# Another order of all steps in an attention and gated-MLP kernel

## The chip, the cores and the metric

One core of a Trainium2 chip runs the whole kernel. The metric is the device time of one execution in microseconds, taken as the median of several runs.

## The reference, cut to what matters

Chunked attention over 4 batches, 8 heads, 768 positions and 64 features; then a gated MLP over the 512 features, whose gate mixes the 768 positions. All in fp32.

```python
for c in range(nc):                       # 24 chunks of 32 queries
    k_ctx = k[:, :, l_start:r_end]        # 16 keys to the left, 8 to the right
    k_full = np.concatenate([mem_k, k_ctx], axis=2)
    scores = scale * np.matmul(q_c, k_full.transpose(0, 1, 3, 2))
    a = softmax(scores)
    out[:, :, c_start:c_end] = np.matmul(a, v_full)
x = attn_out.transpose(0, 2, 1, 3).reshape(B, S, H * D)
h = gelu(x @ w_in)
u, v = h[..., :d_ff // 2], h[..., d_ff // 2:]
v_n = (v - mu) / np.sqrt(var + 1e-06) * g_ln
v_s = np.einsum('ts,bsd->btd', w_sg, v_n) + b_sg[None, :, None]
return x + (u * v_s) @ w_out
```

## The kernel before, in words

The work is cut into some 1,200 named steps. Each step belongs to one engine, or may be put on either of two (a star after its name picks the second). The string ORDER (line 35) lists all steps, and the loop at line 565 issues them in that order. Every engine runs its own steps strictly in the order of the string; semaphores are set by the tiles that a step reads and writes. So the string alone sets the queue of each engine and which buffer a step gets.

The matrix products are made of two fp32r parts each (a high part and the rest), three products for one: low by high, high by low, high by high (`HL`).

- Weights. `r` loads a block of 128 rows of w_in (i) or w_out (o) as 64-bit words, `d1` to `d6` turn it into a high part (`d5`) and a low part (`d6`). i10 to i13 are the four blocks for the V products, i00 to i03 those for the U products. `g`, `ga`, `gb` load and split w_sg. `cb` loads g_ln (in pieces of 4 bytes) and b_sg; `cbh` halves them.
- Attention, for each of 24 tiles of 128 positions (u = 0 to 23, six to a batch): `q`, `k`, `v` load, `S` is the score product (64 small matmuls in the trace, PSUM tile `s`, one buffer), then `mx`, `sb` (VectorE), `ex` (ScalarE), `sm`, `sr`, `nm`. For u < 10 `T` transposes on TensorE and `p` copies; for the others `yt` transposes on VectorE and four `E` steps exchange blocks by 16 DMAs, for two tiles together. `A` is the value product (PSUM tile `av`, one buffer); `xc`, `xh`, `xl` copy it out, as fp32, high and low part.
- MLP, for each batch b: `V` (6 products, by tile), `v1` to `v9` are gelu, layer norm and split (`v1` to `v4` read PSUM; the result lies in one of two `g` buffers from `v1` to `v9`); `U` (8 products), `u1` to `u4` gelu; `W` (8 products, each over all six V results of the batch), `w1` to `w4` scale, gate and split; `O` (8 products), `o1` adds x, `out` stores.
- V, U, W, O and T share four PSUM banks `mm`, given out in the order of the string.
- `zz n` are n warm-up matmuls on a zeroed tile whose result nobody reads.

Names: S13 is the score product of tile 13; V14 is batch 1, tile 4; U103 is batch 1, half 0, column block 3; v714 is step v7 of V14.

The SP queue issues all DMAs in the order of the string; each issue may wait for its buffer.

```python
def warm(n):
    for _ in range(n if mms.free else 0):
        tensor.matmul(mms.free[0], still[:, 0, 0:P], still[:, 1], start=True, stop=True)
```

Of the kernel before, what the change touches and what calls it, by code (L numbers as in the profile page):

```python
# [45 lines left out]
p5 g00 d3o0 xh4 U001 q9 v801 mx7 z6 k9 vy02 gb20 xl4 sb7 v901 u1003 A5 sm6 ex7 u2003 v602 v103 S8 v8 sr6 sm7
nm6* u3003 V04 v203 xc5 k10 q10 xh5 sr7 mx8 v303 xl5 ga11 v403 ga00 gb11 u4003 V05 v503 u1001 v702 u2001 v802
vx03 gb00* u3001 sb8 v902 T6 u4001 ex8 S9 p6 gb01* v104 sm8 nm7* U011 q11 k11 mx9 vy03 v204 v603 sb9 v703*
v304 T7 sr8 u1011 v404 A6 p7 nm8 v803 U013 v504 ex9 v9 v903 xc6 u2011 vx04 sm9 u3011 vy04 v105 v604 u4011 T8
u1013 sr9 v704* v205 A7 p8 u2013 v305 nm9 U010 xc7 v10 v405 v804 u3013 gb50* v505 T9 v904* u1010 A8 u2010 d1o0  # L50
# [5 lines left out]
O003 mx12 w3011 sb12 w4011 k14 q14 ex12 O001 Eb5 o1003 z12 sm12 sr12 nm12 O011 o1001 out003 Ed5 O002 o1011
out011 out001 O013 o1002 yt12 out002 O010 o1013 out013 S13 o1010 out010 O000 mx13 q15 k15 sb13 ex13 S14 sm13
xh6 xh8 o1000 O012 k16 sr13 xh7 mx14 xl8 out000 q16 xl7* xl6* V11 nm13 o1012 yt13 out012 xc9 sb14 xh9 V10 ex14
xl9 v111 sm14 v211 sr14 v311 nm14 S15 v411 v110 v511 A10 q17 v210 k17 U102 vx11 mx15 xc10 v13 vy11 v611 v310
sb15 xh10 v410 ex15 xl10* V13 u1102 v510 u2102 vx10 sm15 u3102 vy10 v610 u4102 sr15 V14 v710 v711 v810 v811  # L60
# [20 lines left out]
yt23 w3213 w1201 w4213* w2201 A20 w1203 w3201 w4201* W212 xc20 v23 w2203 w3203 w4203 O202 w1212 w2212 w3212
w4212 A21 o1202 out202 O200 Eb11 O203 o1200 Ea11 W210 o1203 out200 out203 Ec11 O201 w1210 w2210 Ed11 w3210
w4210* W211 xh19 o1201 xh20 xl19 out201 xh18 xl20* xl18 V31 w1211 w2211 xc21 w3211 w4211* O212 v131 v231 v331
O211 v431 o1212 v531 out212 vx31 V30 vy31 o1211 v631 out211 v731 v831 v931* A22 v130 v230 O210 xc22 v330 v430
v530 U303 o1210 vx30 out210 vy30 v630 v730 U300 u1303 v830 u2303 v930* u3303 u4303 O213 u1300 u2300 u3300
# [548 lines left out]
```

## Time and profile before

| what | us |
|---|---|
| median of 3 runs | 397.53 (397.05 to 400.51) |
| profiled execution | 396.41 |
| its span, first to last instruction | 394.6 |
| TensorE busy in the span | 375.0 |
| VectorE, ScalarE, GpSimd busy | 268.0, 155.0, 111.3 |

In the profile PE is TensorE, PEld its weight loads, DVE VectorE, ACT ScalarE, POOL GpSimd, SPq the queue that issues DMAs. Nearly every step has line 105, since one helper records them all; a group is told by its tiles. Ends of matmuls are modelled, so starts are the better measure for them.

### The profile page before, as it was taken

Reading aid. Unit: us, or ns where it says so; the run is one execution under the profiler, and the core shown is the slowest. Engines: PE = TensorE matmul, PEld = TensorE weight load, DVE = VectorE, ACT = ScalarE, POOL = GpSimd, SP = SyncE. Lnnn points to the kernel's source line nnn. Section 1 sums busy time; section 2 is a strip of 40 time slices with the busy share of each in tenths; the row PEclk is TensorE's granted clock in tenths of the full one; section 3 lists DMA queues with packets and bytes.
Section 4 is the critical chain, followed back from the end, with each engine's and each line's share of the span. In section 5 each row is a group of like instructions: output and inputs, shape, how many; then the busy total and the mean of one; then the engine's idle time right before and its main releaser. Section 6 shows DMA issues by size and latency. Waiting matters only on the chain.

```text
span 394.6 us, 11079 instructions
## 1 busy us (share of the span) xinstructions
PE 375.0 (95%) x4787; PEld 343.7 (87%) x4787; DVE 268.0 (68%) x489; ACT 155.0 (39%) x288; POOL 111.3 (28%) x132
## 2 busy tenths in 40 slices
...
GB/s 261 404 398 218 275 227 182 175 281 119 1 122 168 122 120 64 107 128 154 95 193 156 75 75 3 98 37 67 73 87 96 42 33 9 2 0 0 2 78 83
DMA packets 24528, 47.64 MB, mean 121 GB/s; under 512 B 4384, under 2 KB 13600, under 8 KB 24480
## 3 DMA queue, kind: packets, MB, share of 16 engines
q1 hardware_dynamic: 24480, 46.94, 36.2%
...
HBM read 36.96 MB, written 6.29 MB: 110 GB/s over the span
## 4 chain that ended last, share of the span: by engine, by line
PE 69%; DVE 9%; POOL 7%; DMA 6%; ACT 4%; issue 2%; SPq 2%; DVEq 0%; ACTq 0%; POOLq 0%
PE mma L105 16%; PE mmc L105 16%; PE mmd L105 15%; PE mmb L105 13%; PE av L105 6%; PE s L105 3%; POOL gb L105 2%; SPq L105 2%; DMA rawe<-in_w_in 2%; POOL ga L105 2%; DMA ub<-in_w_sgT 2%; DVE ga L105 2%; DMA ka<-in_ks 1%; DVE paira L105 1%; DVE gb L105 1%
## 5 line engine op out<-in xcount | busy, mean ns | idle before, releaser
L105 ACT ACTIVATE eb<-eb 128x512 f32<-128x512 f32 x12 | 7.6, 631 | 31.4 <-DVE eb L105 31.1
L105 DVE STREAM_TRANSPOSE y<-na 128x512 f32<-128x512 f32 x14 | 9.9, 707 | 6.9 <-DMA pt<-y 3.2
L105 PE MATMUL s<-ka,qa 64*32 64x64 f32 x768 | 10.5, 224 | 3.9 <-DMA ka<-in_ks 2.0
L105 DVE SCALAR_TENSOR_TENSOR mmc<-mmc,g_half,b_half 128x384 f32<-128x384 f32 x11 | 6.8, 621 | 10.7 <-PE mmc L105 10.7
L105 PEld LDWEIGHTS s<-ka,qa 64*32 64x32 f32 x768 | 8.5, 105 | 6.4 <-issue 3.9
L105 PEld LDWEIGHTS av<-pt,vb 64*64 64x64 f32 x512 | 8.8, 134 | 5.8 <-issue 2.5
L105 PE MATMUL av<-pt,vb 64*64 64x32 f32 x512 | 9.8, 221 | 3.5 <-ACT xa L105 1.5
L105 PE MATMUL mma<-w_in_hi,paira 128*128 128x512 f32 x40 | 11.1, 399 | 1.8 <-DVE paira L105 1.8
L105 PE MATMUL mma<-vhf 128*128 128x512 f32 x34 | 10.6, 469 | 2.4 <-POOL vhf L105 2.4
L105 PEld LDWEIGHTS s<-kb,qb 64*32 64x32 f32 x768 | 8.4, 105 | 3.5 <-issue 1.7
L105 PEld LDWEIGHTS mma<-vhf 128*128 128x128 f32 x34 | 7.6, 233 | 4.2 <-POOL vhf L105 2.3
L105 ACT ACTIVATE ea<-ea 128x512 f32<-128x512 f32 x12 | 7.6, 632 | 9.4 <-DVE ea L105 9.4
L105 PE MATMUL s<-kb,qb 64*32 64x64 f32 x768 | 10.5, 224 | 0.7 <-issue 0.7
L105 PEld LDWEIGHTS av<-pt,va 64*64 64x64 f32 x512 | 8.5, 134 | 3.0 <-issue 1.8
L105 PE MATMUL av<-pt,va 64*64 64x32 f32 x512 | 9.5, 221 | 1.2 <-issue 0.8
L105 PEld LDWEIGHTS mma<-w_in_hi,paira 128*128 128x128 f32 x40 | 7.3, 187 | 3.6 <-DVE paira L105 2.1
L105 PEld LDWEIGHTS av<-pt,vc 64*64 64x64 f32 x512 | 8.4, 134 | 2.0 <-issue 1.3
L105 PE MATMUL mma<-w_in_hi,pairb 128*128 128x512 f32 x32 | 8.9, 400 | 1.1 <-DVE pairb L105 1.1
L105 ACT ACTIVATE gb<-gb 128x512 f32<-128x512 f32 x12 | 7.6, 633 | 5.4 <-DVE gb L105 5.4
L105 ACT ACTIVATE ga<-ga 128x512 f32<-128x512 f32 x12 | 7.6, 633 | 5.4 <-DVE ga L105 5.4
L105 DVE SCALAR_TENSOR_TENSOR mmd<-mmd,g_half,b_half 128x384 f32<-128x384 f32 x8 | 5.0, 624 | 6.9 <-PE mmd L105 6.9
L105 PE MATMUL av<-pt,vc 64*64 64x32 f32 x512 | 9.4, 221 | 0.1
(520 smaller groups left out, 1235.2 us busy)
## 6 DMA issues: line engine op xcount, KB each, us to landing
...
pt<-y SPq DMA_DIRECT2D x112, 32.0 KB, 1.9
...
```

Source lines behind the costliest of these rows:

```text
L105: return self.tc.keep_in_program_order(getattr(self.engine, name)(*args, **kw))
```

## The change: another string

Only ORDER changes; the steps are the same. Of the steps that may go on either of two engines 88 change their engine, so VectorE runs 473 steps instead of 489 and GpSimd 138 instead of 122. The warm-up matmuls are 56 instead of 43, in seven pieces. Cut to its beginning and the lines that the text speaks of:

```diff
-g40 ri10 ri13 g10 q0 k0 ri12 k1 g30 d2i10 d1i10 q1 d3i10 d4i10 d2i13* g50 ri00 d1i13 d3i13 d5i10 ri11 d4i13
-d6i10* d5i13 zz17 S0 v0 d6i13 mx0 d2i12* q2 sb0 d1i12 k2 d3i12 ex0 ri02 d4i12 zz9 S1 v1 z0 d5i12 sm0 ri01
-d6i12 mx1 sr0 sb1 d1i00 k3 nm0 d2i00* ex1 d1i11* q3 zz8 T0 d2i11* sm1 p0 sr1 v2 d3i00 zz2 A0 g31 d3i11 d4i00
-xh0 S2 ri03 d4i11 xc0 d5i00 xl0 nm1* q4 d5i11 mx2 d1i02 d6i00 zz4 T1 sb2 d2i02* p1* ex2 d6i11* zz3 A1 k4 sm2
-d3i02 V00 xc1 g51 sr2 d1i01 d2i01 nm2 g41 xh1 d3i01 v3 d4i02 T2 d4i01 d5i02 ro0 S3 p2 xl1 d5i01 A2 mx3 v100
-d6i02 k5 sb3 V01 xh2 v200 xc2 q5 d2i03 v300 xl2 cb ex3 d3i03 d1i03 v400 V02 v101 d4i03 v500 d5i03 v5 sm3 d6i03
-v4 v201 vx00 sr3 S4 v301 d6i01* v401 vy00 ga40 U000 q6 v600 ga31 mx4 ga30 k6 nm3 d2o0* v501 gb30 ga10 T3 ga51
-sb4 ga41 U002 gb10 vx01 g01 ex4 p3 gb40* g21 ga50 sm4 gb51 g20 S5 sr4 v700 u1000 A3 gb31* k7 v800 u2000 q7
...
-vx05 u4013 u3010 vy05 ro1 S10 v605 p9* xc8 v11 v705 U012 k12 u4010 q12 v805 mx10 d4o0 A9 sb10 d5o0 v905* ex10
-S11 v12 d6o0* d1o1 sm10 W012 q13 mx11 k13 d2o1 sb11 sr10 d3o1 ex11 nm10 ro2 W003 w1012 z11 sm11 d4o1 sr11 d5o1
...
-v713* u1101 u4103 u2101 vx14 u3101 vy14 v614 v813 u4101 v714 A11 v913 v814 S16 xc11 v14 v914* Ed6 v112 U100
-mx16 xh11 v212 xl11* v312 sb16 V15 k18 u1100 v412 Eb6 ex16 u2100 v512 u3100 sm16 vx12 u4100 U113 Ea6 vy12 v115
...
-w2100 W113 q21 mx19 v16 w3100 q20 w4100* k20 u1110 Ed7 u2110 u3110 W102 w1113 u4110 k21 w2113 Ea7 w2110 w3113
-w3110 w4113 W103 w1102 w4110* w2102 w3102 w4102* yt16 W111 w1103 nm17 w2103 sb19 w3103 yt17 w4103 ex19 S20
...
-out102 Ea8 O111 o1112 out112 O101 o1111 out111 yt18 nm19* O110 o1101 yt19 out101 sb21 nm20 O100 ex21 o1110
-sm21 out110 sr21 S22 o1100 xh12 xh13 out100 xl12* O113 xh14 xl13 mx22 xl14* sb22 V22 o1113 ex22 out113 xc15
...
-u1212 u4211 v824 u2212 v525 u3212 v924* U213 u1210 vx25 u4212 vy25 v625 u2210 yt20 u3210 v725 A18 u4210 v825
-nm21 S23 xc18 v21 v925 yt21 A19 mx23 nm22* sb23 W213 xc19 Eb10 ex23 z23 sm23 sr23 Ed10 W202 w1213 Ec10 W200
...
-v933* V35 u1302 v434 u3301 u2302 v534 u3302 u4301 u4302 U311 v135 vx34 vy34 v634 v235 v734 v335 U310 v834 v435
...
-u3312 W300 u4312 W303 w1300 w2300 w3300 w4300* u1313 u2313 W311 w1303 u3313 w2303 u4313 w3303 w4303 W301 w1311
...
+k1 ri12 q0 k0 g00 g31 q1 ri13 g30 d2i12 d1i12 ri11 d3i12 v0 d4i12 d5i12 zz18 S0 ri01 d6i12 g11 mx0 k2 sb0 g01
+ex0 zz5 S1 z0 mx1 d1i13 q2 d2i13 sm0 ri10 d3i13 sr0 d4i13 d1i11 v1 sb1 d5i13 nm0 ex1 k3 d2i11 zz17 T0 sm1
+d6i13 p0 sr1 zz2 A0 d3i11 d2i01* q3 nm1 ri03 d1i01 d3i01 T1 xc0 d4i11 cb xh0 d4i01 p1 d5i11 zz3 S2 ri00 xl0
+d5i01 d6i11* mx2 d6i01 d1i10 q4 d2i10* sb2 zz5 A1 v2 d3i10 ex2 d4i10 ri02 sm2 d5i10 xc1 sr2 d6i10 xh1 zz6 S3
+k4 xl1* nm2* V00 mx3 d1i03 q5 d2i03 v3 sb3 cbh g50 ex3 sm3 d2i00* g21 T2 sr3 V01 d1i00 k5 d3i03 p2 d3i00 v100
+d4i03 v200 nm3* d5i03 ro0 A2 v300 d4i00 v101 v400 v4 d6i03 T3 d2i02* v201 xh2 S4 v5 d1i02 v500 xc2 xl2 p3 vx00
+d3i02 V02 d5i00 q6 mx4 vy00 v301 v600 sb4 d6i00 k6 v401 ex4 d4i02 A3 sm4 d5i02 v700 S5 xc3 v6 sr4 d6i02* v800
+q7 mx5 nm4* U000 ga01 k7 v501 d2o0* v900 ga30 sb5 ga31 vx01 ex5 d3o0 T4 ga50 U001 gb30* v102 gb01* ga21 g10
...
+d5o0 v705 A7 d6o0 v805 S9 xc7 v10 v905 A8 mx9 q11 k11 sb9 d1o1* W000 xc8 v11 ex9 sm9 d2o1 sr9 d3o1 nm9 ro2
...
+ex15 v211 sm15 v311 sr15 v411 A10 v112 v511 S16 v212 xc10 v13 vx11 v312 A11 vy11 mx16 k18 v611 q18 v412 V10
...
+sb17 u3103 yt15 ex17 u4103 nm16* U111 z17 v114 sm17 v214 sr17 v314 V15 u1111 v414 u2111 v514 u3111 u4111 vx14
...
+u3100 u4100 W103 Ec7 Eb7 W111 w1103 w2103 w3103 w4103 v16 u1102 W101 w1111 u2102 w2111 u3102 w3111 u4102 yt16
+w4111* W113 w1101 nm17* w2101 yt17 w3101 sb19 nm18* ex19 S20 w4101* sm19 A14 q22 w1113 k22 sr19 w2113 W112
...
+yt19 xh14 o1101 xh12 sb21 xh13 out101 xl14* ex21 xl13 S22 o1111 sm21 out111 V22 mx22 sr21 nm20 xc15 xl12* xh15
+sb22 V21 xl15 v122 ex22 v222 sm22 v322 sr22 v422 V20 v522 v121 v221 vx22 v321 vy22 v622 v421 v722* A16 v521
+vx21 S23 xc16 v19 vy21 v822 A17 v621 mx23 xh16 v721 V23 xl16* xc17 v20 Ed9 v821 v922* xh17 v921* v120 xl17
+v220 V24 Eb9 v320 v123 v420 v223 v520 v323 Ea9 vx20 v423 U212 vy20 v620 v523 v720* Ec9 V25 u1212 u2212 v820
+vx23 vy23 u3212 v623 u4212 v920 U200 v723 v124 v823 v224 v923 U202 v324 yt20 u1200 v424 nm21* v125 u2200 U211
...
+u3211 A18 u1201 sr23 v525 u4211 U213 v824 v21 vx25 u2201 xc18 vy25 v625 u4202 u3201 v924* u4201 v725* U203
+u1213 yt21 u2213 u3213 nm22* v825 u4213 A19 u1203 v925 u2203 U210 xc19 Ec10 u3203 u4203 W210 Eb10 Ea10 W201
...
+V35 v833 v434 u1303 v933 v534 u2303 vx34 u3303 vy34 v634 u4303 U310 v135 v734 v235 v834 v934* v335 U312 v435
...
+u3311 W313 u4311 W311 w1313 W310 w1311 w2311 w3311 w4311 u1313 W302 w1310 u2313 w2310 u3313 w3310 u4313 w4310*
...
```

## Rows read from the trace of the kernel before

**Rows 1.** The page, part 1: busy time, share of the span and instructions of each engine.

```profile
PE 375.0 (95%) x4787; PEld 343.7 (87%) x4787; DVE 268.0 (68%) x489; ACT 155.0 (39%) x288; POOL 111.3 (28%) x132
```

**Rows 2.** Windows of 2 us: PE, PEld, DVE, ACT, POOL busy; clock, DMA, GB/s.

```profile
26.00:28.00 2.00, 1.45 (x24) 1.23 (x25) 2.00 (x6) 0.85 (x2) 0.00 (x0) 0.77 1.03 391
...
28.00:30.00 2.00, 2.00 (x6) 1.61 (x5) 1.04 (x2) 1.34 (x3) 1.10 (x1) 0.50 1.06 391
...
36.00:38.00 2.00, 2.00 (x10) 1.60 (x9) 2.00 (x5) 1.65 (x4) 0.00 (x0) 1.00 0.65 90
```

**Rows 3.** Timeline of TensorE, start to 60 us: start, duration, what, idle before.

```profile
10.47 0.85 PE L105 MATMUL s<-ka,qa 64*32 64x64 f32 x64 [2.00 <-DMA ka<-in_ks]
...
26.55 0.55 PE L105 MATMUL av<-pt,vb 64*64 64x32 f32 x22 [1.26 <-issue]
...
27.02 2.04 PE L105 MATMUL mmc<-w_in_hi,paira 128*128 128x512 f32 x4
...
40.76 0.97 PE L105 MATMUL mmd<-paira,w_in_lo 128*128 128x384 f32 x4
...
42.97 0.60 PE L105 MATMUL mmc<-ident,na 128*128 128x128 f32 x4
```

**Rows 4.** Timeline of the other engines, start to 25 us; the same columns.

```profile
14.09 0.69 DVE L105 TENSOR_REDUCE rda<-ea 128x8 f32<-128x520 f32 x1
...
14.72 0.69 DVE L105 TENSOR_REDUCE mxb<-s 128x8 f32<-128x512 f32 x1
...
18.45 1.28 POOL L105 TENSOR_TENSOR na<-eb,rdb 128x512 f32<-128x512 f32 x1
...
18.75 1.53 DVE L105 SCALAR_TENSOR_TENSOR exb<-rawb,exb 128x512 int32<-128x512 int32 x1
```

**Rows 5.** Chain that ended last, in order of time: start, us, what.

```profile
8.72 6.81 DMA rawe<-in_w_in
...
27.09 4.54 PE mmc L105 x12
...
37.24 2.80 PE mmb L105 x12
...
40.04 0.79 PE s L105 x53
...
46.44 1.06 PE av L105 x64
...
101.22 3.18 PE mma L105 x18
...
118.00 2.08 PE mmc L105 x12
```

**Rows 6.** Windows of 40 to 80 us and of 85 to 391 us; columns as in rows 2.

```profile
40.00:80.00 40.00, 39.70 (x975) 35.11 (x978) 38.77 (x76) 30.93 (x62) 28.82 (x32) 1.00 0.65 208
...
85.00:391.00 306.00, 298.63 (x3135) 279.96 (x3128) 196.53 (x357) 100.02 (x186) 69.86 (x81) 1.00 0.26 80
```

**Rows 7.** Timeline, 79 to 82 us: U012 on TensorE and v705 on VectorE.

```profile
80.19 0.55 DVE L105 TENSOR_SCALAR gb<-gb,mvc,rsc 128x512 f32<-128x512 f32 x1
...
80.22 0.96 PE L105 MATMUL mma<-pairb,w_in_lo 128*128 128x384 f32 x4
```

**Rows 8.** Timeline of TensorE after 150 us: rows ahead of which it sat idle.

```profile
158.55 0.73 PE L105 MATMUL mma<-w_in_hi,pairb 128*128 128x512 f32 x2 [1.13 <-DVE pairb L105]
...
194.97 0.86 PE L105 MATMUL s<-ka,qa 64*32 64x64 f32 x64 [1.06 <-DVE eb L105]
...
225.56 0.73 PE L105 MATMUL mma<-w_in_hi,paira 128*128 128x512 f32 x2 [1.82 <-DVE paira L105]
...
266.50 1.14 PE L105 MATMUL av<-pt,vb 64*64 64x32 f32 x64 [1.50 <-ACT xa L105]
```

**Rows 9.** Timeline, 228 to 238 us: first and last step after V22.

```profile
228.65 0.60 ACT L105 ACTIVATE gb<-mma 128x512 f32<-128x512 f32 x1 [0.75 <-PE mma L105]
...
236.48 0.69 DVE L105 TENSOR_TENSOR vhc<-gb,vhc 128x512 fp32r<-128x512 f32 x1 [0.36 <-ACT vhc L105]
```

More of the change, by code (lines that the diff above doesn't have):

```diff
@@ L46 @@
[L46 to L50, printed above, removed]
@@ L56 @@
[L56 to L60, printed above, removed]
@@ L71 @@
-out102 Ea8 O111 o1112 out112 O101 o1111 out111 yt18 nm19* O110 o1101 yt19 out101 sb21 nm20 O100 ex21 o1110
-sm21 out110 sr21 S22 o1100 xh12 xh13 out100 xl12* O113 xh14 xl13 mx22 xl14* sb22 V22 o1113 ex22 out113 xc15
-sm22 xh15 sr22 xl15* A16 v122 v222 U201 xc16 v19 v322 xh16 v422 xl16 v522 V21 u1201 vx22 u2201 vy22 v622 u3201
-v722* u4201 V23 v121 v822 v221 v922* v321 v421 U200 v521 v123 v223 vx21 v323 vy21 v621 V20 v423 u1200 v721*
-u2200 u3200 v821 u4200 v921* U202 v120 v220 v320 A17 u1202 v420 u2202 U203 xc17 Ea9 v520 u3202 vx20 xh17 v523
@@ L76 @@
-vy20 v620 u4202 v720* V24 xl17* u1203 v20 u2203 Ec9 vx23 v820 vy23 v623 u3203 v920 u4203 V25 Ed9 v723* v124
-v224 v823 v324 v923* U211 Eb9 v424 v125 v524 v225 U212 u1211 vx24 v325 vy24 u2211 v624 v425 u3211 v724 U210
-u1212 u4211 v824 u2212 v525 u3212 v924* U213 u1210 vx25 u4212 vy25 v625 u2210 yt20 u3210 v725 A18 u4210 v825
-nm21 S23 xc18 v21 v925 yt21 A19 mx23 nm22* sb23 W213 xc19 Eb10 ex23 z23 sm23 sr23 Ed10 W202 w1213 Ec10 W200
-w1202 w2202 Ea10 w3202 w4202 u1213 W201 w1200 v22 u2213 w2200 u3213 yt22 w3200 w4200* u4213 W203 nm23 w2213
@@ L81 @@
[L81 to L85, printed above, removed]
@@ new lines @@
+q7 mx5 nm4* U000 ga01 k7 v501 d2o0* v900 ga30 sb5 ga31 vx01 ex5 d3o0 T4 ga50 U001 gb30* v102 gb01* ga21 g10
+xh3 v202 z5 g51 gb31 ga00 xl3* p4 gb00 sm5 g41 S6 ga11 v302 sr5 nm5 V03 g20 k8 v402 gb50 mx6 vy01 q8 u1001
+v502 gb11 u2001 gb21 u1000 vx02 T5 sb6 u3001 A4 u2000 ex6 vy02 g40 v601 u4001 ga10 z6 S7 u3000 v701* v7 sm6
+xc4 u4000 U003 k9 ga51 mx7 q9 xh4 sr6 p5 sb7 gb10 ga20 xl4 v801 U002 gb20* u1003 v901* ex7 u2003 ga40 v602
+v103 sm7 gb51 S8 u3003 v203 u1002 gb40 u4003 A5 ga41 k10 mx8 v303 q10 v702* sr7 V04 v403 xc5 v8 xh5 u2002 v503
@@ new lines @@
+u3002 xl5 v802 gb41* u4002 V05 v902* vx03 nm6 v104 vy03 v204 v603 sb8 v304 U011 v703 ex8 v404 v803 sm8 v903
+v504 T6 u1011 sr8 U012 vx04 p6 nm7* u2011 v105 u3011 vy04 v205 v604 u4011 v305 T7 v704 A6 u1012 v405 nm8* v804
+u2012 U013 xc6 v9 v505 u3012 v904* u4012 d1o0* p7* T8 u1013 vx05 U010 p8 u2013 vy05 ro1 d4o0 u3013 v605 u4013
+d5o0 v705 A7 d6o0 v805 S9 xc7 v10 v905 A8 mx9 q11 k11 sb9 d1o1* W000 xc8 v11 ex9 sm9 d2o1 sr9 d3o1 nm9 ro2
+W011 w1000 d4o1 w2000 d5o1 w3000 d6o1 W001 w1011 w4000 d1o2 w2011 d2o2 w3011 d3o2 u1010 u2010 ro3 d4o2 u3010
@@ new lines @@
+W003 w1001 d5o2 u4010 d6o2* w2001 w4011* w3001 S10 w4001 w1003 d1o3 w2003 T9 q12 mx10 W002 k12 w3003 p9* sb10
+w4003* ex10 d2o3 sm10 S11 d3o3 w1002 A9 k13 sr10 w2002 q13 nm10* mx11 w3002 W012 v12 w4002* yt10 sb11 d4o3
+ex11 d5o3 z11 sm11 S12 d6o3 w1012 W013 k14 mx12 q14 w2012 sb12 w3012 sr11 w4012 ex12 nm11* S13 w1013 z12 yt11
+O001 q15 k15 mx13 Ea5 sm12 sb13 O003 o1001 ex13 sr12 w2013 nm12* Ec5 sm13 w3013 w4013* O002 o1003 sr13 out003
+Ed5 S14 o1002 W010 mx14 sb14 out002 ex14 out001 sm14 Eb5 sr14 S15 w1010 w2010 O000 mx15 k17 w3010 q16 w4010*
@@ new lines @@
+k16 q17 O011 o1000 xh7 xh6 out000 xl7* xh8 xl6 yt12 V11 o1011 xl8 out011 nm13 yt13 V12 xc9 sb15 nm14* v111
+ex15 v211 sm15 v311 sr15 v411 A10 v112 v511 S16 v212 xc10 v13 vx11 v312 A11 vy11 mx16 k18 v611 q18 v412 V10
+xc11 v14 v711 Ed6 v512 v811 sb16 v911 vx12 ex16 sm16 vy12 U101 Eb6 v612 v110 sr16 v712 v210 v812 v310 v912*
+O010 u1101 v410 Ea6 u2101 v510 u3101 O013 u4101 o1010 vx10 out010 vy10 v610 Ec6 O012 v710 o1013 v810 v910
+out013 U103 o1012 xh11 xh10 out012 xl11 xh9 xl9* S17 xl10 u1103 yt14 A12 q19 mx17 k19 nm15* V14 u2103 v15 xc12
@@ new lines @@
+sb17 u3103 yt15 ex17 u4103 nm16* U111 z17 v114 sm17 v214 sr17 v314 V15 u1111 v414 u2111 v514 u3111 u4111 vx14
+vy14 U110 v115 v614 v714 v215 v814 v315 v914 V13 u1110 v415 u2110 v515 u3110 u4110 vx15 S18 v113 vy15 v615
+v213 U113 q20 k20 v715 v313 mx18 v815 v413 U112 v915* u1113 v513 sb18 vx13 u2113 ex18 vy13 S19 v613 u1112 z18
+u3113 A13 v713* u2112 q21 mx19 k21 u3112 U100 u4113 xc13 Ed7 u4112 sm18 v813 sr18 v913* U102 u1100 Ea7 u2100
+u3100 u4100 W103 Ec7 Eb7 W111 w1103 w2103 w3103 w4103 v16 u1102 W101 w1111 u2102 w2111 u3102 w3111 u4102 yt16
@@ new lines @@
+w4111* W113 w1101 nm17* w2101 yt17 w3101 sb19 nm18* ex19 S20 w4101* sm19 A14 q22 w1113 k22 sr19 w2113 W112
+xc14 v17 mx20 w3113 sb20 w4113 ex20 sm20 sr20 W110 w1112 w2112 w3112 w4112 W100 w1110 w2110 w3110 w4110* O112
+w1100 w2100 w3100 w4100 A15 o1112 out112 S21 Ed8 W102 mx21 Ea8 O110 w1102 w2102 k23 v18 w3102 q23 w4102* O113
+Eb8 o1110 O100 o1113 out110 Ec8 O102 o1100 out100 out113 O103 o1102 out102 O101 o1103 yt18 out103 nm19 O111
+yt19 xh14 o1101 xh12 sb21 xh13 out101 xl14* ex21 xl13 S22 o1111 sm21 out111 V22 mx22 sr21 nm20 xc15 xl12* xh15
@@ new lines @@
+u3211 A18 u1201 sr23 v525 u4211 U213 v824 v21 vx25 u2201 xc18 vy25 v625 u4202 u3201 v924* u4201 v725* U203
+u1213 yt21 u2213 u3213 nm22* v825 u4213 A19 u1203 v925 u2203 U210 xc19 Ec10 u3203 u4203 W210 Eb10 Ea10 W201
+w1210 Ed10 W202 w1201 w2201 v22 w3201 w4201* u1210 u2210 W203 w1202 u3210 yt22 w2202 nm23 w3202 u4210 w4202
+A20 yt23 w2210 W212 w1203 xc20 v23 w3210 w2203 w4210 w3203 w4203 W200 w1212 w2212 w3212 w4212 A21 w1200 w2200
+W213 Ec11 w3200 w4200 Eb11 O200 w1213 w2213 w3213 Ea11 w4213* O201 o1200 out200 O203 o1201 Ed11 O202 o1203
@@ new lines @@
+out201 out203 W211 o1202 xh20 xh18 out202 xl20 xh19 xl19 V32 w1211 xl18 w2211 xc21 w3211 w4211 U302 v132 v232
+v332 O210 v432 u1302 u2302 v532 u3302 u4302 O213 o1210 vx32 out210 vy32 v632 v732* U300 o1213 out213 v832 O212
+u1300 v932* u2300 u3300 V31 u4300 o1212 out212 V30 v131 v231 v331 v431 O211 v531 v130 v230 vx31 v330 vy31 v631
+U301 v430 xh21 o1211 v731 out211 xl21* v831 A22 v530 u1301 v931 u2301 V33 vx30 xc22 vy30 u3301 v630 xh22 u4301
+v730* xl22* A23 v133 v830 v233 V34 xc23 v930* v333 xh23 v433 xl23 v533 vx33 U303 vy33 v134 v633 v234 v733 v334
```

22 lines of the change are left out of this document (5 added, 17 removed).

## The prediction

> **What bounds the kernel now.** I read the page's busy times first, then windows, then the timeline of TensorE, then the chain that ended last. TensorE is busy for 375.0 of 394.6 us, VectorE for 268.0, GpSimd for 111.3 [rows 1]. The change computes the same products, so the time can move in only three places: the head before TensorE has steady work, the pauses inside, and the tail. The tail is one add and one store in both orders.
>
> The head: the first score product S0 starts at 10.47, after a wait for k0; the first V product V00 starts at 27.02 [rows 3]. In between TensorE does three scores, two transposes, two value products and warm-up products. The DMA queues are full (share 1.03 to 1.06 and 391 GB/s at 26 to 30 us, [rows 2]), VectorE and ScalarE split the weights and run the softmax chain, and the granted clock falls: 0.77 at 26 to 28 us and 0.50 at 28 to 30 [rows 2]. V00 took 4.54 us where V02 took 2.80 [rows 5], so the half clock cost 1.7.
>
> The middle: between 40 and 80 us TensorE is busy 39.70 of 40 us and VectorE 38.77 [rows 6]. There both are the bound; a step saved on one is worth nothing if the other is late.
>
> The rest: from 85 to 391 us TensorE is busy 298.63 of 306 us [rows 6]. The 7.37 us of pauses are what a better order could win there. Four of them hold 5.51: V15 (1.13, for its input's low part), S20 (1.06, for sb19), V22 (1.82, low part), A19 (1.50, for xc18) [rows 8].
>
> **Prices.** A score product 0.79, a value product 1.06, V 2.80, U or O 2.08, W 3.18 [rows 5]; transposes at most 0.60 [rows 3]. VectorE starts one 512-wide step 0.63 after another (14.09 to 14.72), a GpSimd step takes 1.28 [rows 4]; I use 0.62 for ScalarE too, since its shapes are the same.
>
> **The change, part by part. The head.** By the diff S0, S1, S2, S3 and A0, A1 precede V00; A2 stands behind V01, so the "three value products" of the summary are two by the lines, and I follow the lines.
>
> Loads: k0 is now the fourth transfer, 1504 KB into the queue and not 2032; at 391 GB/s (382 KB per us) that is 1.4 us, so S0 starts near 9.1 (sizes by the shapes: 256 KB for a q, 368 for a k, 512 for a v or a weight block, 192 for a g). Against this, the last of the four weight blocks that V00 needs (ri10) stands 5904 KB in, where ri11 stood 4576 KB in. Block ri00, 4064 KB in, landed at 8.72 + 6.81 = 15.53 [rows 5]; 1840 KB more puts ri10 at 20.4.
>
> Then the engines, step after step in their queues. S0 9.1; mx0, sb0 to 11.4; S1 11.5; VectorE runs mx1, d2i13, sm0, d3i13, sr0, d4i13, sb1 before nm0, which ends at 17.1; zz17 covers TensorE until then. T0 17.2, p0 to 18.7, A0 18.8. A0 and A1 pause in mid-product for nothing that the profile shows (A1: 1.26 us, [rows 3]); I leave such a pause in both. xc0, xh0 to 22.2, xl0 22.9, p1 and d5i11 to 23.4, d6i11* 24.1, mx2, sb2 25.4, d3i10, d4i10 26.7 (the 27th step of VectorE), d5i10 27.4, d6i10 on GpSimd 28.8. V00 needs d5i10 for its first product and d6i10 for its fifth: start 27.5, a wait of about 0.4, end 30.7 at full clock. Before, V00 ended at 27.09 + 4.54 = 31.6 [rows 5]. The four zz pieces after T0 fill what before was idle, so I take the full clock; the half clock again would cost 1.7 on V00, most of it hidden by the next wait.
>
> That wait: V01 30.9 to 34.0, A2 35.0, T3 and S4 36.2, then V02 must have xl2. On ScalarE xh2 stands behind ex3, d2i00*, d1i00, p2, v100, d5i03, v300, v101 and d2i02*; from 31.0 that is ten steps, to 37.5. xl2 ends at 38.3, V02 starts at 38.4 (before: 37.24 by the chain, [rows 5]). After V02 (41.2), A3 and S5, U000 starts at 43.1. Before, U000 started at 40.76 with one score, one value product and one transpose less done ahead of it: 40.76 + 0.79 + 1.06 + 0.5 = 43.1 [rows 3, 5]. **So the head is worth 0**: the earlier S0 and the saved half clock go into the wait for xl2. The other bounds: if xl2 comes in time the head wins 2.2; if cb, now moved up among the weight loads, holds up k4, k5 and ri02, it loses up to 2. For cb the row is 36 to 38 us, where its small pieces flowed: 90 GB/s at a DMA share of 0.65 [rows 2], so two or three us of the queue.
>
> **The middle.** Ahead of W000 the new order has the same products as the old one ahead of U012, but one U more, one S and one T less: 80.22 + 2.08 - 0.79 - 0.4 = 81.1 is where the old pace would start W000 [rows 5, 7]. VectorE: W000 needs V05's chain; v705 is the 120th step of VectorE and was the 124th, which ran at 80.19 [rows 7]. At 0.52 us a step (38.77 us for 76, [rows 6]) it comes at 78.1; then v805, and v905, moved to GpSimd (1.28): 80.6. Also A8 must wait for xc7, which ScalarE holds behind v805: 79.9, against A8 due at 80.0. Both engines arrive together, with under 1 us to spare; I take +0.4 for the middle.
>
> One row speaks against the change. VectorE's d3i11 took 1.53 us while nm1* ran on GpSimd beside it; its neighbours take 0.69 [rows 4]. The new order moves 16 steps net from VectorE to GpSimd (473 and 138 by the order), three of them ahead of W000: 3 x 0.84 = 2.5 us at worst, 0 at best; this is inside the +0.4 and its upper bound. The Trainium skill, page SBUF — State Buffer, section "Who interferes with whom", says that a VectorE step with two SBUF inputs and a GpSimd step that reads SBUF shut each other out for a whole instruction; this one row agrees. By that rule every moved step could hold up VectorE, 16 x 0.84 = 13 us of its time, by estimate, most of it where VectorE has slack.
>
> **The rest.** Each of the four pauses has its cause in the order, and the new order takes the cause away. V15 now stands some 20 us of products behind A11. S20's sb19 stood behind yt16, which waits for the E7 transfers; the last of these, Ea7, was issued one W product ahead of it, behind k20 and k21 on the SP queue; now two W products (6.4 us) lie between the last, Eb7, and yt16. V22's low part (xl14*) stood behind yt19, sb21, nm20, sm21, sr21 and mx22 on VectorE; now behind yt19, o1101 and sb21, with O111 and S22 (2.9) as cover. xc18 stood behind v825; now two U products (4.2) lie between it and A19. What I find new: A11 and A17 have only one score (0.79) ahead of them for their copy of 0.6 (0.3 each), S20 still has 0.5, W313 has 8.3 us of products for V35's chain as W300 had (0.5). With 1.0 for what I don't see: 2.6 in place of 7.37, **-4.8**. Bounds: 0.5 left (-7) and all 7.4 back (0).
>
> **Sum.** 394.6 + 0 + 0.4 - 4.8 = 390.2 for the span. The profiled execution took 396.41, 1.8 over its span, and the median of the runs is 397.53, 1.1 over that: **393.1**.
>
> **The rivals.** *The pauses move but don't go (no change).* Every wait that I removed is replaced by one of the same kind, as xc7 behind v805 copies xc18 behind v825. For it: 95% of the span is filled already [rows 1], and an order that fills one place takes cover from another. Then -4.8 becomes -1: 397. *The head's lead lasts.* If xl2 isn't late, V02 starts at 36.3 and the middle keeps 2.2: 391. *Two g buffers become the bound (slower).* A V product's result holds one of two buffers from v1 to v9, 228.65 to 237.17 for V22, 8.5 us [rows 9], and its PSUM bank until v4. For batch 2 the new order puts V22, V21 and V20 back to back, with v722*, v721 and v720* in the chain; V24's bank is free about 0.9 us before U211 asks for it. It decides at a chain of 9.5 us: at 10.5 to 11, three rounds in batch 2 lose 5 us and W103 and W313, with 11.0 and 8.3 us of cover, 2 each: 393 + 9 = 402.
>
> *The clock.* Rows 2 show half clock after a stretch with little done. The Trainium skill, page TensorE: Matmul & The Clock Gate, section "HAM oscillation — how this bites in real kernels", says that waits between groups of matmuls bring the clock down again and again; the trace shows one fall, in the head. By that rule the wait for xl2 would cost V02 another 1.7, by estimate.
>
> **How the numbers follow.** Forecast 393.1 (392 to 395.5): 0.45. Pauses replaced, 397: 0.25. Head's lead kept, 391: 0.18. Buffers as the bound, 402: 0.12. For 8 in 10 the range runs from 388.5 (lead kept and 0.5 left of the pauses) to 400 (pauses back, middle late by 2.5). Within 1%, about what a measurement can tell from no change, means 393.6 to 401.5: faster 0.48 (half of the forecast's case and the lead), same 0.39, slower 0.13.
>
> **What would show it.** S0 near 9 us, V00 near 27.5 and no clock of 0.50 under it; V02 at 38 to 39 behind xl2; W000 at 81 to 82; TensorE idle for 2 to 4 us between W000 and the last product. The prediction is wrong if W000 starts past 84, or if the pauses after it exceed 6 us.

## The result, and the profile after

The changed kernel takes 394.59 us (median of 16 executions, 391.70 to 398.26), the kernel before on the same chip 398.15 (395.53 to 401.62): a ratio of 0.990 with an interval of 0.987 to 0.993. The profiled execution took 391.93, its span is 390.0. The forecast was 393.1, with a span of 390.2. The sum came out; two of its terms did not. The profiled execution lies 2.7 us below the median of its kernel; that of a second trace ("changed, again", 394.90) is nearer to it.

The page, part 1, of the changed kernel (busy time of each engine, share, instructions):

```profile
PE 374.6 (96%) x4800; PEld 344.7 (88%) x4800; DVE 259.9 (67%) x473; ACT 155.1 (40%) x288; POOL 130.6 (33%) x148
```

Against [rows 1] TensorE does the same work, and 13 warm-up matmuls more, in 4.6 us less span, and 8 us of VectorE's work are now on GpSimd, where they take 19. Next, the timeline of TensorE (start, duration, what, idle before): S0, V00, V02, U000, V05, W000 and the last product.

```profile
8.71 0.85 PE L105 MATMUL s<-ka,qa 64*32 64x64 f32 x64 [0.27 <-DMA ka<-in_ks]
...
26.54 1.19 PE L105 MATMUL mmc<-w_in_hi,paira 128*128 128x512 f32 x4
...
38.45 0.73 PE L105 MATMUL mmd<-w_in_hi,paira 128*128 128x512 f32 x2 [3.18 <-DVE paira L105]
...
43.30 0.62 PE L105 MATMUL mmc<-paira,w_in_lo 128*128 128x384 f32 x2
...
66.47 1.29 PE L105 MATMUL mma<-w_in_hi,pairb 128*128 128x512 f32 x4 [2.24 <-DVE pairb L105]
...
84.85 0.44 PE L105 MATMUL mmc<-w_sg_hi,vha 128*128 128x384 f32 x1
...
384.83 1.55 PE L105 MATMUL mmd<-paira,w_out_hi 128*128 128x384 f32 x8
```

S0, V00 and U000 answer to [rows 3]: S0 is 1.8 us earlier than before, V00 0.5 earlier and U000 2.5 later, all near the forecast (9.1, 27.5, 43.1). Then comes what was not: V05 stands 2.24 us behind its input's low part, and W000 is at 84.85 where the old pace has 81.1. The last product ends at 386.38, 301.5 us later. For comparison the last rows of TensorE in the kernel before:

```profile
388.90 0.86 PE L105 MATMUL mmd<-pairb,w_out_lo 128*128 128x384 f32 x4
389.59 1.55 PE L105 MATMUL mmd<-pairb,w_out_hi 128*128 128x384 f32 x8
```

There the end was 391.14, so the same stretch took 310.0. **The middle lost 3.7 us (forecast 0.4), the rest won 8.5 (forecast 4.8), and the two errors cancelled.** In the second pair of traces they are 4.5 and 5.8. Windows of the changed kernel; columns as in rows 2:

```profile
67.00:69.00 2.00, 2.00 (x7) 1.54 (x6) 1.94 (x5) 0.60 (x1) 0.79 (x2) 0.61 0.00 0
69.00:71.00 2.00, 2.00 (x7) 1.58 (x6) 2.00 (x5) 1.60 (x3) 0.35 (x1) 0.54 0.00 0
40.00:80.00 40.00, 37.16 (x661) 32.54 (x660) 37.51 (x69) 27.09 (x55) 25.78 (x27) 0.96 0.46 143
84.85:386.40 301.55, 299.98 (x3331) 282.66 (x3324) 190.27 (x351) 102.66 (x190) 84.48 (x95) 1.00 0.28 89
```

From W000 on TensorE is idle for 1.57 us of 301.55, against 7.37 of 306 in [rows 6]. In the middle it is idle for 2.84 of 40 (before 0.30), and a fall of the granted clock from full (2.4 GHz) to half (1.2 GHz) lies under V05, which takes 4.61 us instead of 2.96; under V00 there is none.

The reason for V05's wait stands one engine further. VectorE and GpSimd in the changed kernel, timeline:

```profile
58.39 2.98 DVE L105 TENSOR_TENSOR vhb<-gb,vhb 128x512 fp32r<-128x512 f32 x1
...
57.93 0.96 POOL L105 TENSOR_TENSOR rsc<-rsc,mhalf 128x1 f32<-128x1 f32 x1
58.87 1.00 POOL L105 TENSOR_TENSOR w_sg_lo<-ue,w_sg_hi 128x384 fp32r<-128x384 f32 x1
59.83 0.98 POOL L105 TENSOR_TENSOR w_sg_lo<-ug,w_sg_hi 128x384 fp32r<-128x384 f32 x1
```

The first is v901*, a step of 0.69 elsewhere ([rows 9], last row). It took 2.98 while three GpSimd steps ran back to back (v602, gb51, gb40) and ended 0.56 behind the last of them. Everything behind it on VectorE, xl5 among it, came 2.3 us later. In the kernel before, v901 ran on GpSimd itself; it is one of the steps that the new string put on VectorE.

The profiled execution of one experiment (four causes moved) was disturbed; only its waits and the times of its other executions are used.

### The profile page after: what moved, and what is told of

It reads as the page before. It is cut to its first block, busy times and chain, and to the rows that moved or that the text cites. A ratio compares the mean times of both kernels' runs of the same rounds, so it can differ in the third digit from the quotient of the medians.

```text
span 390.0 us, 11100 instructions
## 1 busy us (share of the span) xinstructions
PE 374.6 (96%) x4800; PEld 344.7 (88%) x4800; DVE 259.9 (67%) x473; ACT 155.1 (40%) x288; POOL 130.6 (33%) x148
## 4 chain that ended last, share of the span: by engine, by line
PE 75%; DVE 13%; ACT 4%; DMA 3%; POOL 1%; issue 1%; SPq 1%; ACTq 0%; DVEq 0%
PE mmc L105 18%; PE mma L105 17%; PE mmd L105 17%; PE mmb L105 16%; PE av L105 4%; PE s L105 3%; DMA ka<-in_ks 2%; DVE gb L105 1%; DMA out<-xa 1%; SPq L105 1%; DVE rdb L105 1%; POOL pairb L105 1%; DVE vhb L105 1%; ACT w_sg_hi L105 1%; DVE na L105 1%
## 5 line engine op out<-in xcount | busy, mean ns | idle before, releaser
L105 DVE SCALAR_TENSOR_TENSOR mma<-mma,g_half,b_half 128x384 f32<-128x384 f32 x8 | 5.0, 623 | 14.6 <-PE mma L105 14.6
L105 PE MATMUL mma<-vhf 128*128 128x512 f32 x40 | 11.7, 449 | 2.3 <-POOL vhf L105 2.3
L105 PEld LDWEIGHTS mma<-vhf 128*128 128x128 f32 x40 | 8.5, 220 | 4.4 <-POOL vhf L105 2.3
L105 PE MATMUL mma<-w_in_hi,pairb 128*128 128x512 f32 x24 | 7.7, 448 | 2.2 <-DVE pairb L105 2.2
L105 PE MATMUL mmd<-w_in_hi,paira 128*128 128x512 f32 x24 | 6.7, 399 | 3.2 <-DVE paira L105 3.2
L105 DVE SCALAR_TENSOR_TENSOR gb<-gb,mmc 128x512 f32<-128x512 f32 x10 | 6.8, 679 | 4.0 <-ACT gb L105 4.0
```

Of the source, the lines that this page charges most:

```text
L105: return self.tc.keep_in_program_order(getattr(self.engine, name)(*args, **kw))
```

## The experiments

All are other strings of the same steps and the same products, but for one product in the last ("old causes back"). In the diffs "..." leaves steps out and | parts two places. "Rest" is the time from W000's start to the last product's end, "to W000" that from S0's start; both take out where the trace happens to begin. In the kernel before, U012's start plus 0.9 stands for W000, as in the prediction.

| kernel | median us | ratio to before (interval) | span | to W000 | rest |
|---|---|---|---|---|---|
| changed | 394.59 | 0.990 (0.987 to 0.993) | 390.0 | 76.1 | 301.5 |
| changed, again | 393.63 | 0.989 (0.983 to 0.995) | 393.0 | 77.1 | 303.8 |
| before, again | 396.69 | 0.999 (0.995 to 1.003) | 394.1 | 70.7 | 309.6 |
| old head, new rest | 393.82 | 0.986 (0.979 to 0.993) | 390.6 | 70.4 | 306.0 |
| new head, old rest | 410.73 | 1.029 (1.023 to 1.035) | 410.8 | | |
| four causes moved in the old order | 394.21 | 0.988 (0.984 to 0.992) | | | |
| two GpSimd steps later | 392.58 | 0.984 (0.979 to 0.990) | 389.4 | 75.0 | 301.8 |
| products in two waits | 396.60 | 0.996 (0.993 to 1.000) | 392.4 | 76.7 | 303.9 |
| xl2 earlier | 393.15 | 0.989 (0.984 to 0.993) | 391.4 | 74.9 | 303.9 |
| xl2 earlier, GpSimd later | 390.24 | 0.982 (0.977 to 0.986) | 388.3 | 72.7 | 303.9 |
| five moves | 390.19 | 0.981 (0.977 to 0.984) | 386.7 | 72.7 | 301.1 |
| middle steps earlier | 389.67 | 0.979 (0.973 to 0.986) | 387.6 | 71.9 | 303.0 |
| old causes back | 396.25 | 0.995 (0.992 to 0.998) | 393.5 | 76.2 | 305.6 |

### Are head and rest separable?

Old head, new rest: the steps ahead of W000 in the old kernel's sequence, then the new string.

```diff
-k1 ri12 q0 k0 ... d5o0 v705 A7 d6o0 v805 S9 xc7 v10 v905 A8 ... W000 xc8
+g40 ri10 ri13 ... d5o0 v905* d6o0* d1o1 u1012 u2012 u3012 u4012 W000 xc8
```

> Steps that stand ahead of W000 in the new order are issued in the old order (with the old 43 warm-up products); from W000 on the new order stands. Theory (head and middle cost, the rest wins, and the two are separate): by the two traces the new order reaches W000 3.7 us later than the old pace (84.85 against 81.1), and needs 301.5 us from there to the last product where the old one needed 310.0. So this kernel ends 3.7 us before the changed one: span 386 to 387, ratio to the kernel before 0.978 to 0.982. Rival (not separate: the rest runs smoothly only because the new head left other chains ready): span 390 to 395, ratio 0.99 to 1.00.

W000 came at 80.97, as expected, but the rest took 306.0, so the rival held for this trace. The lead went ahead of S11 and W002 (waits of 1.3), and at A10, for which the timeline shows its copy's buffer as the reason:

```profile
132.58 0.59 ACT L105 COPY xa<-av 128x512 f32<-128x512 f32 x1 [7.07 <-DMA out<-xa]
...
133.22 1.29 PE L105 MATMUL av<-pt,vb 64*64 64x32 f32 x64 [1.75 <-ACT xa L105]
```

xc9 waits until an older output has been stored from x's buffer, and A10 for xc9. In the changed kernel A10 waited 0.42, but in its second trace, with the same string, 1.29:

```profile
135.49 1.29 PE L105 MATMUL av<-pt,vb 64*64 64x32 f32 x64 [1.29 <-ACT xa L105]
```

So A10's wait changes from one execution to the next (0.4 to 2.2 in the traces with the new rest, none in one), and only part of it can be put down to the old head. Behind it the clock was 0.50 from 136 to 140 us, which cost V10 alone 1.5. By the median this kernel can't be told from the changed one (0.986 and 0.990).

The opposite half, the new string as far as the old kernel's W012 has work done, then the old one:

```diff
-d3o3 w1002 A9 k13 sr10 w2002 ... W012 v12 w4002*
+p9* sb10 ex10 sm10 S11 A9 v12 W012 q13 mx11 k13
```

> Steps that stand ahead of W012 in the old order are issued in the new order (with the new 56 warm-up products); from W012 on the old order stands. Theory: the loss of the middle alone, span 398 (394.6 + 3.7), ratio 1.007 to 1.012; the pauses at V22, A19, S20 and V15 stand as before (TensorE idle 6 to 8 us after W012). Rival (not separate): span 392 to 395, ratio 0.99 to 1.00.

Both numbers were missed by 12 us and more. The seam itself cost it: waits ahead of T9 and S11 and half clock between 91 and 100 us. What it keeps is that v901* took 2.99 in it too, and V05 waited 2.25: that loss belongs to the new head. And the four pauses stand in it as in the kernel before (V15 1.46, S20 1.28, V22 1.80, A19 1.52): they belong to the old rest.

### The middle

Two GpSimd steps moved from v901*'s side:

```diff
-v103 sm7 gb51 S8 u3003 v203 u1002 gb40 u4003 ... V05 v902* vx03
+v103 sm7 S8 u3003 v203 u1002 u4003 ... V05 v902* gb51 gb40 vx03
```

> The new order with two GpSimd steps (gb51, gb40) moved behind v902*; the queues of TensorE, VectorE and ScalarE stay as they are. Theory (GpSimd shuts VectorE out: v901* took 2.98 us beside three GpSimd steps, xl5 came 2.3 late, V05 waited 2.24 and then ran at half clock): v901* 0.7 to 1.0, V05 at 64 to 64.5, no clock of 0.5 in its products, W000 at 81 to 82, span 386 to 387.5, ratio 0.979 to 0.985. Rival 1 (VectorE's queue is too full in any case): v901* short, but W000 at 83.5 to 85 and span 389 to 390. Rival 2 (the 2.98 us have another cause): v901* stays at 2.5 to 3 us and the span at 390.

VectorE's v901*, GpSimd's v602 and TensorE's V05 in it:

```profile
61.31 0.68 DVE L105 TENSOR_TENSOR vhb<-gb,vhb 128x512 fp32r<-128x512 f32 x1
...
60.83 0.98 POOL L105 TENSOR_TENSOR rsc<-rsc,mhalf 128x1 f32<-128x1 f32 x1
...
67.12 1.19 PE L105 MATMUL mma<-w_in_hi,pairb 128*128 128x512 f32 x4
```

The step is back to 0.68, V05 has no wait and no half clock, and it is so in all four traces with these two steps moved; in the six with them in their place v901* took 2.98 to 3.04. So the two GpSimd steps were the cause. v602 still runs beside v901* in this trace, so it alone doesn't hold it up. The gain was only 1.1 us to W000, since here the clock fell under V02, behind its wait for xl2, for another 2.6:

```profile
39.00:41.00 2.00, 2.00 (x6) 1.52 (x6) 1.90 (x4) 0.72 (x2) 1.92 (x3) 0.50 0.58 215
```

W000 (83.95) and the span (389.4) are so the numbers of rival 1, but not by its mechanism, since V05 waits for nothing.

Does the wait itself bring the clock down? One more warm-up product of nine matmuls ahead of V02, one ahead of V05:

```diff
-d3i02 V02 d5i00 ... u4002 V05 v902*
+d3i02 zz9 V02 d5i00 ... u4002 zz9 V05 v902*
```

> The changed kernel with one warm-up product more ahead of V02 (in TensorE's wait for xl2, 3.25 us) and one more ahead of V05 (in the wait for xl5, 2.5 us). Nothing that the reference asks for changes. Theory, that V05's half clock (1.66 us) follows from TensorE standing still before it: no stretch at clock 0.5 between 30 and 85 us, the waits themselves as long as they were, W000 at 83.2 to 83.6 us instead of 84.85, span 388.4 against 390.0. Rival, only the waits count and the clock under V05 has another reason: clock 0.5 at V05 again, W000 at 84.8, span 390.

The windows of 67 to 71 us in it, and A8's last row:

```profile
67.00:69.00 2.00, 2.00 (x10) 1.64 (x9) 1.95 (x5) 0.60 (x1) 0.87 (x2) 1.00 0.00 0
69.00:71.00 2.00, 2.00 (x12) 1.91 (x12) 2.00 (x5) 1.69 (x3) 0.27 (x1) 1.00 0.00 0
```

```profile
84.82 0.19 PE L105 MATMUL av<-pt,vc 64*64 64x32 f32 x1 [1.53 <-issue]
```

No half clock, as the theory had it, and yet W000 at 84.94: the 1.6 us saved were lost inside A8, in front of its last matmul, to a pause for which the trace names no releaser. A17 lost 0.94 in the same way. Where such pauses stand follows a count. Over all traces, those over 0.2 us inside a product have 222, 349, 476, 603, 984, 1111, 1493, 1618 or 3649 matmuls ahead of them: whole multiples of 127 apart to within 2, in the old strings and the new. In the changed kernel the place behind 1493 matmuls is in W000; the 18 matmuls more move it into A8, and in the new head with the old rest it is in S10, which paused there too (0.37). Why the pauses come at that distance is open.

One trace doesn't show that the products kept the clock up: the run with xl2 earlier has none ahead of V05, a wait of 2.27 and no fall. The ratio to the kernel before is 0.7% higher than that of the changed kernel, and the two intervals don't overlap. Filling waits with products is no cure here.

xl2 earlier, alone and with the GpSimd steps later:

```diff
-ro0 A2 v300 d4i00 v101 ... v201 xh2 S4 v5 d1i02 v500 xc2 xl2 p3
+ro0 A2 xh2 xl2 v300 d4i00 v101 ... v201 S4 v5 d1i02 v500 xc2 p3
```

> The changed kernel with xh2 and xl2 placed right behind A2 in the order of the steps, instead of behind the steps that the new order puts first. Theory, that V02 waits for xl2 alone: V02 starts at 35.5 to 36 us instead of 38.45 (A2 ends at 33.9), TensorE's wait there falls from 3.25 to under 1 us, and W000 comes at 82 to 83, span 387.5 to 388.5. Rival, that VectorE bounds the middle: V02 starts earlier but W000 is still at 84 to 85, span 389.5 to 390, since v901 still stands in the stretch of GpSimd.

> Both moves at once: xh2 and xl2 right behind A2, and the two GpSimd steps gb51 and gb40 behind v902, so that v901 doesn't run beside them. Theory, that the two waits (for xl2, for xl5) are the whole loss of the middle: W000 at 81 us (the old kernel's own pace point), the rest as in the changed kernel (301.5), end at 382.5 and span 384 to 387. Rival, the time taken out at one place comes back at the next wait (A8, W002, V12) or as half clock: span 388 to 390.

U000, V03, V05 and W000 of the first, then V02 and W000 of the second:

```profile
43.62 0.62 PE L105 MATMUL mmc<-paira,w_in_lo 128*128 128x384 f32 x2 [1.33 <-DVE w_in_lo L105]
...
50.07 1.17 PE L105 MATMUL mmb<-w_in_hi,pairb 128*128 128x512 f32 x4 [1.12 <-DVE pairb L105]
...
67.04 1.19 PE L105 MATMUL mma<-w_in_hi,pairb 128*128 128x512 f32 x4 [2.27 <-DVE pairb L105]
...
83.86 0.44 PE L105 MATMUL mmc<-w_sg_hi,vha 128*128 128x384 f32 x1
```

```profile
36.56 1.20 PE L105 MATMUL mmd<-w_in_hi,paira 128*128 128x512 f32 x4
...
80.81 0.44 PE L105 MATMUL mmc<-w_sg_hi,vha 128*128 128x384 f32 x1
```

With xl2 alone V02 starts earlier (36.83), but U000's wait for w_in_lo and V03's for pairb, which stand behind it, take that back before V04 begins. The wait of V05 is as long as ever (2.27); the 1.2 us gained to W000 are the half clock that didn't come under V05 here. W000 (83.86) is nearest the rival's 84, and the span (391.4) is past both forecasts.

Both moves together bring 3.4, and W000 to 80.81 where 81 was expected. Since U000 and V03 wait again (0.81 and 1.10), what this adds to the GpSimd steps' move is that no half clock came under V02; in the four traces with xl2 earlier none did. That it can't come there without the wait is not shown. So the middle's loss is shown to be v901*'s delay and the half clock behind a wait; xl2's part in it is argued.

The rest is 2.4 longer than in the first trace of the changed kernel: 1.0 of it at A10 (1.46 for 0.42), 1.4 at W113, O111 and S22. That gives the rival's span, 388.3, but it isn't shown that the moves did this: the changed kernel's second trace has 303.8 too, with more time at the same four products. Against the kernel before its interval lies wholly below that of the changed kernel.

### Further along the same way

Against what those traces still showed, four moves more, then three more:

```diff
-xh7 xh6 out000 xl7* xh8 xl6 yt12 V11 o1011 xl8 | A10 v112 v511 S16 v212 xc10 | Ea6 ... Ec6 | A7 d6o0 v805 S9 xc7
+xh7 xh8 xh6 out000 xl7* xl8 xl6 yt12 V11 o1011 | A10 xc10 v112 v511 S16 v212 | Ea6 Ec6 ... | A7 xc7 d6o0 v805 S9
```

> The two moves of the run before, and four more against the pauses that were left in the changed kernel: xh8 and xl8 ahead of xh6 and xl6 (V12's wait, 0.58 us in the changed kernel and 1.91 in the one with the old head), xc10 right behind A10 (A11's, 0.84), Ec6 right behind Ea6 (A12's, 0.69), xc7 right behind A7 (A8's, 0.6). Theory, that each pause goes with its late step: after W000 0.5 to 1 us of pauses instead of 2.6, span 382 to 385, ratio to the kernel before 0.970 to 0.978. Rival, that pauses move to other steps, as O113's did to V22: span as in the run before, within 1 us.

```diff
-mx4 ... ex4 d4i02 A3 sm4 d5i02 ... xc3 v6 sr4 d6i02* ... mx5 ... gb30* ... xh3 ... xl3* | xl10
+d4i02 mx4 ... d5i02 ex4 A3 d6i02* sm4 ... xc3 xh3 ... mx5 xl3* ... gb30* | xl10*
```

> The kernel with five groups of moves, and three more against what its trace showed: d4i02, d5i02 and d6i02* ahead of mx4, ex4 and sm4 (U000's wait for w_in_lo, 1.0 us), xh3 right behind xc3 and xl3* right behind mx5 (V03's wait for pairb, 1.1), xl10 on VectorE instead of GpSimd (V14's wait, 0.8). Theory, that each pause goes and that the middle isn't bound by VectorE's sum of work: W000 2 us earlier as counted from S0 (70.6 instead of 72.65), 1 us less behind it, span 383 to 384.5, ratio 0.972 to 0.975. Rival, that VectorE sets W000 through v705, which stays where it was because no work leaves VectorE ahead of it: W000 at 72 to 73 from S0, span 386 to 387.

Neither is distinguishable from the one before it (0.981, 0.979 after 0.982). Single pauses went as meant: with xc10 moved, A11's fell from 0.76 to 0.23. Others took their place. V14's wait in "five moves", then S5's in "middle steps earlier":

```profile
150.49 1.20 PE L105 MATMUL mmb<-w_in_hi,pairb 128*128 128x512 f32 x4 [0.83 <-POOL pairb L105]
```

```profile
41.79 0.86 PE L105 MATMUL s<-kb,qb 64*32 64x64 f32 x64 [1.36 <-DVE ea L105]
```

S5 now waits for sb4, which stands behind the steps that I had moved up. One expectation named a wrong cause: what I had called V12's wait is A10's, for xc9 behind the store of out000, as the rows of the old head show, and xl8 has no part in it. Moving out000 ahead of the loads q16, k16 and q17 on the SP queue wasn't tried.

### The rest

Old order, four late steps earlier:

```diff
-A11 v913 v814 S16 xc11 ... xh11 v212 xl11* | W102 ... Ed7 ... Ea7 | xh14 xl13 mx22 xl14* | A18 u4210 v825 nm21 S23 xc18
+A11 xc11 xh11 xl11* v913 v814 S16 | W113 Ed7 Ea7 ... W102 | S22 xh14 xl14* ... xl13 mx22 | A18 xc18 u4210 v825 nm21 S23
```

> The old order with eight steps moved, for the four pauses of V15, S20, V22 and A19: xc11, xh11, xl11* right behind A11; Ed7, Ea7 right behind W113; xh14, xl14* right behind S22; xc18 right behind A18. Theory (each pause has its cause in the order of one queue): the four pauses shrink from 5.5 to under 1.5 us, span 390 to 391, ratio 0.988 to 0.992. Rival (pauses move to the next place): the same idle time elsewhere, span 393.5 to 395, ratio 0.997 to 1.002.

The time is that of the theory (0.988), and so eight steps moved in the old order give as much as the whole new string (0.990). Of the waits for the four causes V15's and V22's are gone and A19's is 0.37 instead of 1.50. But A12 waits 0.96 for its transposed input, A16 0.80 for the copy xc15, and S20 2.35, now for k20's load behind the E transfers. The theory had under 1.5 for the four; S20's alone is longer, so the time was met but not by the waits as forecast.

The changed kernel with three of the old late steps:

```diff
-xl14* ex21 xl13 S22 ... V22 mx22 sr21 nm20 xc15 | Ea7 ... Ec7 Eb7 W111 ... u1102 W101 | xc18 vx25 ... v825 u4213
+ex21 xl13 S22 ... V22 mx22 sr21 nm20 xl14* xc15 | W111 ... u1102 Ea7 Ec7 Eb7 W101 | vx25 ... v825 xc18 u4213
```

> The changed kernel with three of the late steps of the old order put back: xl14* behind mx22, sr21 and nm20 on VectorE (before: V22 late by 1.82 us), xc18 behind v825 on ScalarE (before: A19 late by 1.50), and Ea7, Ec7 and Eb7 issued only ahead of W101 instead of one and two W products earlier (before: S20 late by 1.06). The same products are computed. Theory, that these steps were the causes: up to W000 nothing changes (84 to 85 us); V22 and A19 wait 1.5 to 2 us each again, S20 0.5 to 1; from W000 to the last product 305 to 306 us instead of 301.5, span 394, ratio to the kernel before about 1.00. Rival, that the new order of the products covers them wherever the steps stand: each wait under 0.5 us, 302 from W000 on, span 390 to 391.

S20, V22 and A19, then xl14* (the first of two steps in its row) on VectorE:

```profile
192.54 0.86 PE L105 MATMUL s<-ka,qa 64*32 64x64 f32 x64
...
227.13 1.20 PE L105 MATMUL mmc<-w_in_hi,paira 128*128 128x512 f32 x4
...
264.61 1.14 PE L105 MATMUL av<-pt,vb 64*64 64x32 f32 x64 [0.80 <-ACT xa L105]
```

```profile
228.86 2.39 DVE L105 TENSOR_TENSOR paira<-xb,paira 128x512 fp32r<-128x512 f32 x2
```

The sums are the theory's (rest 305.6, ratio 0.995), the mechanism isn't. Only A19 waits again (0.80); S20 doesn't wait. For V22 this run shows nothing: its string has xl14* behind V22 itself, so V22 doesn't wait for that low part but reads the one that w4100 to w4103 left in the buffer, and xl14* ends 2.4 us after V22's start. That one product is not the one that was asked for, against the expectation's "the same products". From V22 on this trace is 1.4 us longer than the changed kernel's; the other 2.6 lie ahead of it, at A10 (1.65) and in half clock from 136 to 142 us, where nothing had been moved.

### What belongs to the order, and what to one execution

> The changed kernel as it is, once more, on the chip of the two others. It tells which of its pauses are those of the order and which are those of one run. By the theory the waits for xl2 (V02) and xl5 (V05) are there again, 3.2 and 2.2 us, and W000 comes at 84 to 85.5; the half clock may be at another place or not there, by 1.5 to 2.7 us. Rival, that the waits belong to the one run: one of the two under 1 us.

> The kernel before as it is, with a second profile. It tells how much of its pauses belong to the order. Theory, that the old order costs what its first trace shows: the same four pauses (V15, S20, V22, A19) within 0.5 us each, the last product 309 to 311 us behind the place that corresponds to W000 (U012's start plus 0.9), half clock at V00 or another product of the head. Rival, that they belong to one run, as the half clock's place does in the changed kernel: two or more of the four gone and others in their place, the same stretch 306 to 308.

The changed kernel again, V02 and V05, then the window at V02's start:

```profile
38.18 1.22 PE L105 MATMUL mmd<-w_in_hi,paira 128*128 128x512 f32 x2 [2.41 <-DVE paira L105]
...
68.69 0.50 PE L105 MATMUL mma<-w_in_hi,pairb 128*128 128x512 f32 x1 [2.29 <-DVE pairb L105]
```

```profile
38.00:40.00 2.00, 1.82 (x4) 1.49 (x5) 1.90 (x5) 0.93 (x2) 1.62 (x3) 0.50 0.71 264
```

Both waits are there again; the half clock is under V02 now (2.6 us) and not under V05. The kernel before, V15, S20, V22 and A19:

```profile
158.32 1.19 PE L105 MATMUL mma<-w_in_hi,pairb 128*128 128x512 f32 x4 [1.13 <-DVE pairb L105]
...
194.42 0.86 PE L105 MATMUL s<-ka,qa 64*32 64x64 f32 x64 [0.73 <-DVE eb L105]
...
224.75 1.20 PE L105 MATMUL mma<-w_in_hi,paira 128*128 128x512 f32 x4 [1.80 <-DVE paira L105]
...
265.71 0.49 PE L105 MATMUL av<-pt,vb 64*64 64x32 f32 x20 [1.51 <-ACT xa L105]
```

These are [rows 8] over again, within 0.4 us, and the rest is 309.6. So these waits belong to the order; the length of A10's and where the clock falls don't. There was no fall at V00 in this trace, and V02 came at 36.66 instead of 37.08: half clock there costs about 0.4, and a pause inside A2, of 1.46 in this trace, hides the rest.

## Why the prediction was right, and where it wasn't

- **The head, worth 0: right, by its steps.** S0, V00, V02 and U000 were within 1 us of their times, U000 within 0.2, and V02 stood behind xl2. With xl2 moved, V02 came 1.6 us earlier. That V02 was right to 0.1 is in part luck: xh2 ended at 36.64 and not 37.5, but xl2 waited until 37.71, for the copy xc2 too, which the prediction didn't have in its way.
- **The middle, +0.4: the term that failed**, at +3.7 and +4.5 in two traces. By the prediction's own mark (W000 past 84) it was wrong there. It had the mechanism, GpSimd steps that hold up VectorE, up to 2.5 us, but spread this over all moved steps and took it for covered. One step in one place took 2.3 of it, and xl5 was next in line with V05 waiting. The prediction took the net of the steps that change engine; of those ahead of W000, 14 went to GpSimd, gb40 among them, and 12 came to VectorE, v901* among them. It counted V05's chain at VectorE's mean pace (0.52 us a step; the row gives 0.51), which put v705 at 78.1 where it started at 81.67, and never followed xl5. The second half of the loss, 1.65 of half clock, was left to a remark.
- **VectorE beside GpSimd.** The Trainium skill, page SBUF — State Buffer, section "Who interferes with whom", says that a VectorE step with two inputs in SBUF and a GpSimd step that reads SBUF shut each other out for a whole instruction. The trace agrees on who is held up (2.98 us beside gb51 and gb40, 0.68 without); the step ended only behind the second of the two, so the wait went past one instruction. The 13 us estimated by its rule didn't come: counting the steps that took over 0.15 us more than the median of their kind, VectorE's excess was 8.7 us in the changed kernel and 7.4 before.
- **The rest, -4.8: right in direction, too small.** It measured 8.5 and, in the second pair of traces, 5.8. The idle time of [rows 6] (7.37) understates what the pauses cost: counted from start to start of the products, against the median of each kind and those over 0.2 us alone, they came to 10.9 us (10.1 in the second trace). The 2.6 left over came out at 2.3 in the first trace and at 4.7 in the second.
- **The four causes.** All four pauses are in every trace that has the old rest as it was, with the old head (twice) and with the new; in the changed kernel's two traces none is over 0.4. A19's late step is shown as its cause: put back, half of the wait returned (0.80 for 1.50). S20's transfers put back brought no wait, so in the new order their place alone doesn't make one; that the products ahead of it cover it is argued. V15 and V22 were tried only in the old order, where their waits went.
- **The rivals.** The two g buffers never became the bound: for V22 to V24 the chain from v1 to v9 took 10.4 us, past the 9.5 at which the prediction had it decide, and yet TensorE has no wait from V22 to U211 in the first trace. "The pauses move" is not what the change did, but it is what every further change did from 0.982 on.
- **The clock.** The Trainium skill, page TensorE: Matmul & The Clock Gate, section "HAM oscillation — how this bites in real kernels", describes a kernel in which every wait between groups of matmuls brings the clock down. Here one of the two waits did so in each trace of the changed kernel, never both, and not the same one; in the run with the new head and the old rest both did; with xl2 earlier the wait of 2.27 us at V05 brought none.
- **The chances.** The 0.48 for "faster" is not the sum it names: half of the forecast's case and the lead give 0.405. The total was right by luck, as two errors of opposite sign (+3.3 and -3.7).
